# Feed-forward weights sent by GpSimd's DMA queue with a cast on the way, a fourth full set of exponentials, and another order

## The chip, the cores and the metric

The kernel runs on one core of a Trainium2 chip. The metric is the device time in microseconds of one launch, as the median of the runs shown; the profiled execution is a run of its own, with its own time. PE is TensorE, DVE VectorE, ACT ScalarE, POOL GpSimd and SP SyncE. The profile's "PEld" is TensorE's weight load, and "SPq" or "ACTq" stands for the DMA issues of that engine's queue.

## The reference

A chunk-selecting attention over 4 batches of 8 heads (768 positions, 64 dimensions a head) is followed by a feed-forward layer with a hard swish. Cut to what matters:

```python
k_min, k_max = chunks of 32 keys: min and max over each chunk
ub = sum over d of max(q * k_min, q * k_max)         # bound of each query on each chunk, causal
top_chunks = the 6 chunks with the largest bound
scores = q @ k.T / 8, kept where the chunk is chosen and the key is not later than the query
attn = softmax(scores) ; a = attn @ v                # float32 in and out
x = a with the 8 heads side by side                  # 3072 x 512
h = x @ w_in                                         # 512 x 2048
out = (h * clip(h + 3, 0, 6) / 6) @ w_out            # 2048 x 512
```

## The kernel before, in words

**Work units.** The 32 (batch, head) pairs are handled as 16 pairs of heads (i = 0 to 15, four to a batch), and from batch 1 on as six "quads" of four heads (n = 2 to 7). The feed-forward layer runs over eight groups g of 384 tokens, two to a batch. All the work is cut into tokens such as `S.1.3.b`, and a list of them, `ORDER`, is written out by hand: each token issues its instructions when its turn comes. Each engine runs its own instructions in the order of the list, and waits on semaphores for what it needs. A DMA is issued by the queue of the engine that is named for it, and stands in that engine's order too.

**Attention of batch 0** (capital letters). `LK`, `LQ`, `LV` load half pairs of k, q and v on SP's queue, `AK` and `AQ` some on ACT's. `KT` and `QT` transpose them on PE; `MX` and `MN` make the chunk bounds on DVE; `UH`, `UB`, `TH`, `T8`, `SE`, `LH`, `MT` make the mask rows from the six largest bounds. `EG` spreads a chunk indicator on POOL. `S.i.u` puts scores and mask of unit u (of six, line 23) of pair i into a two-bank PSUM tile, `ex` takes the exponential on ACT into a bf16 tile `PT`, `af` cuts the diagonal on POOL, `A` and `B` multiply with v, `na` and `nb` normalise on DVE into `XB`. `VC` casts v on POOL.

**Attention of batches 1 to 3.** `lk.n` and `lq.n` load a quad as four DMAs each into a third of `STAGE` in rows of 64 floats; `kd`/`qd` transpose 32 by 32 on DVE, `kb`/`qb` cast on ACT, `mx`, `mn`, `kx`, `rp` make the bounds' operands, `ud` the bounds on PE, `us`, `tr`, `tm`, `se`, `tb` the mask on DVE, `mv` gathers the mask rows on POOL (16 small copies a quad), `SQ` the scores.

**Feed-forward.** `X`/`xe` (batch 0) or `xt` (a transposing DMA) lay x out. `H.g.f` is 8 matmuls of 384 columns; it needs the 512 columns of w_in that hold f, that is chunk f // 2. `hu` (ACT) and `gt` (DVE) are the gate. `O.g.t.n` is 4 matmuls of 512 columns with chunk n of w_out; `ot` copies the result out on ACT and `st` stores it on SP. The last tile, g = 7 and t = 2, is `last_project`: two halves of 256 columns, each with its own copy and store; `st.7.1` is issued on SP behind them.

**Weights.** w_in and w_out come as eight chunks of 1 MB of float32 (n = 0 to 3 for w_in, 4 to 7 for w_out). `wl.n` (line 233) loads a chunk on SP's queue into one of two staging tiles `WS`, and `wc.n` (line 237) casts it on POOL into the bf16 matrices `WIN` and `WOUT`. A load waits for the cast two chunks before it, and a cast waits in POOL's order. The space of `WOUT` is lent to `RN` (line 198) while batch 0's bounds are made.

**Exponentials.** Three full sets of `PT` are tiles of their own. The fourth lies in the two `WS` tiles, and is used from pair 4 on, when the weights are cast; pairs 0 to 3 go round three sets (lines 182 to 188).

Of the kernel before, what the change touches and what calls it, by code (L numbers as in the profile page):

```python
# [39 lines left out]
SE.1.0 LH.1.0.a ex.0.0 MN.1.1 MX.1.1 MT.1.0 TH.2.0.y T8.2.0 SE.2.0 LK.0.1.1 KB.1.1 KT.0.1.x KB.0.1 LK.2.1.1 UH.1.1.a  # L40
LQ.0.1.1 UB.1.1 S.1.1.c ex.1.1 LK.2.1.0 KT.2.1.b KB.2.1 LQ.3.0.1 MN.0.1 LQ.0.1.0 QT.0.1.a MX.0.1 RA.0.1 LK.3.0.0
LK.3.0.1 LH.2.0.c QT.3.0.y QB.0.1 MT.2.0 MN.2.1 RP.0.1 RN.3.0 MX.2.1 LV.0.0.1 KT.3.0.x MN.3.0 QB.3.0 MX.3.0 S.2.1.c
RP.3.0 ex.2.1 af.2.1 LQ.2.1.1 S.1.0.a ex.1.0 UH.0.1.b LK.3.1.0 KB.3.0 TH.1.1.y LQ.2.1.0 UB.0.1 T8.1.1 SE.1.1 S.2.0.b
ex.2.0 UH.3.0.c QT.2.1.a RP.2.1 bd UB.3.0 RA.2.1 LQ.3.1.0 LQ.3.1.1 QT.3.1.x LH.1.1.c af.0.0 MT.1.1 QB.2.1 lk.2
TH.0.1.y S.1.3.b UH.2.1.c QB.3.1 af.1.0 ex.1.3 T8.0.1 SE.0.1 S.1.2.a ex.1.2 UB.2.1 RN.3.1 TH.3.0.y LH.0.1.c LV.0.0.0
MT.0.1 TH.2.1.b LK.3.1.1 T8.3.0 SE.3.0 S.0.3.c RP.3.1 ex.0.3 T8.2.1 S.0.2.a LV.1.0.0 ex.0.2 LH.3.0.y MT.3.0 KT.3.1.x
SE.2.1 MN.3.1 VC.0.0 A.0.y na.0 S.3.1.c af.1.2 ex.3.1 S.0.4.b ex.0.4 LV.1.0.1 VC.1.0 LV.3.0.1 MX.3.1 S.0.5.a ex.0.5
LH.2.1.c MT.2.1 af.1.1 LV.3.0.0 LV.2.0.1 A.1.y UH.3.1.c KB.3.1 na.1 LV.2.0.0 UB.3.1 S.2.5.b ex.2.5 af.0.2 VC.2.0
S.3.0.a kd.2.0 LV.0.1.1 ex.3.0 X.0.0.x VC.3.0 af.2.0 TH.3.1.y S.1.5.c ex.1.5 S.2.3.b ex.2.3 xe.0.0 T8.3.1 A.2.x
af.0.3 SE.3.1 S.1.4.a na.2 LV.0.1.0 S.2.2.c ex.1.4 LV.1.1.0 LH.3.1.x kd.2.1 MT.3.1 ex.2.2 af.0.5 VC.0.1 B.0.0.y  # L50
af.3.0 B.0.1.y nb.0 af.3.1 A.3.x LV.1.1.1 wl.0 LV.3.1.1 S.3.2.b na.3 ex.3.2 af.1.5 S.3.5.a ex.3.5 S.3.3.c X.0.1.y
xe.0.1 S.3.4.b ex.3.4 mn.2.0 af.1.3 VC.1.1 B.1.0.x B.1.1.x mn.2.1 ex.3.3 LV.2.1.1 nb.1 S.2.4.a ex.2.4 af.2.3 wc.0
H.0.0.b mx.2.1 LV.2.1.0 X.1.0.c VC.2.1 af.3.2 af.2.5 af.2.2 B.2.0.x mx.2.0 hu.0.0 af.3.5 LV.3.1.0 VC.3.1 gt.0.0
B.2.1.x wl.1 nb.2 af.3.3 B.3.0.y B.3.1.y H.0.1.b nb.3 X.1.1.x wc.1 kx.2 kb.2.1 xe.1.0 xe.1.1 hu.0.1 H.0.3.a gt.0.1
lk.3 kd.3.0 hu.0.3 gt.0.3 kd.3.1 H.1.3.c hu.1.3 H.1.2.b hu.1.2 gt.1.3 wl.2 H.0.2.a gt.1.2 wc.2 hu.0.2 H.0.5.c hu.0.5
mn.3.1 gt.0.2 gt.0.5 H.1.5.b hu.1.5 wl.3 wc.3 mx.3.1 H.0.4.a hu.0.4 H.0.7.c hu.0.7 gt.1.5 lq.2 kb.2.0 gt.0.4 kb.3.1
H.1.1.b hu.1.1 wl.4 wc.4 qd.2.1 rp.2.1 gt.0.7 qd.2.0 wl.5 rp.2.0 gt.1.1 mx.3.0 H.0.6.c hu.0.6 gt.0.6 mn.3.0 ud.2.b.a
O.0.0.0.y qb.2.0 us.2.1 us.2.0 O.0.2.0.x qb.2.1 tr.2.1 lq.3 H.1.6.b tr.2.0 hu.1.6 tm.2.1 tm.2.0 se.2.1 kx.3 wc.5
O.0.2.1.x tb.2.1 mv.2.3 H.1.4.a kb.3.0 hu.1.4 se.2.0 gt.1.6 O.0.0.1.y tb.2.0 qd.3.1 H.1.7.b rp.3.1 qd.3.0 rp.3.0
# [635 lines left out]
```

## Time and profile before

| what | value |
|---|---|
| median of 3 runs (range) | 274.97 us (274.05 to 279.04) |
| profiled execution, its own time | 274.82 us |
| its span, first to last instruction | 273.1 us |
| granted TensorE clock, mean | 0.997 |
| PE busy | 258.8 us, 95% of the span |
| DVE, ACT, POOL busy | 180.8, 180.4, 104.0 us |
| moved by DMA | 36.47 MB, 134 GB/s over the span |

Of the profiled execution's time, 1.7 us (274.82 less 273.1) lie outside the span. In the views, a row of windows gives the busy time of each engine in a stretch with the number of instructions in brackets, the granted clock, the DMA share (1 is all 16 engines busy; packets that overlap take it above 1) and GB/s. A row of the timeline gives start, length, engine, line and operation, and in square brackets the idle time before it with what ended it. A wait row gives the total in us, the number of times and the longest.

### The profile page before, as it was taken

What the parts mean: (1) busy time and instruction counts of PE and PEld (TensorE: products, weight loads), DVE (VectorE), ACT (ScalarE), POOL (GpSimd) and SP (SyncE); (2) the same over time, 40 slices, a digit from 0 to 9 for tenths busy, and PEclk for the clock granted to TensorE, in tenths of its full rate; (3) what the DMA queues carried; (4) which work ended last, traced back from release to release, by engine and by line L of the source; (5) the groups of instructions that cost most, each with busy time, mean ns of one, the idle gap of its engine ahead of it and who ended that gap; (6) DMA issues with size and microseconds to landing.
All of it is one profiled execution on the core that took longest, in us unless ns stands there. A gap on an engine that the chain in (4) does not pass through costs nothing.

```text
span 273.1 us, 8672 instructions
## 1 busy us (share of the span) xinstructions
PE 258.8 (95%) x3594; PEld 151.2 (55%) x3594; DVE 180.8 (66%) x450; ACT 180.4 (66%) x249; POOL 104.0 (38%) x243
## 2 busy tenths in 40 slices
PE   6899999779799999999999999999999999999994
PEld 2576786445444655755546754556565555555553
DVE  5998989979879596978866775555864212442340
ACT  3699984584499779958878673787577743435441
POOL 6525764424938756408354063322173120000000
PEclk9999999999999999999999999999999999999998
DMA  9978899999996957399912607540410240522103
GB/s 168 199 165 179 242 246 266 217 334 282 252 194 149 241 99 158 90 129 197 215 63 67 127 5 154 125 89 2 108 34 2 77 60 0 118 59 77 41 0 115
DMA packets 93111, 36.47 MB, mean 134 GB/s; under 512 B 85776, under 2 KB 86032, under 8 KB 93072
## 3 DMA queue, kind: packets, MB, share of 16 engines
q1 hardware_dynamic: 90672, 35.33, 58.7%
q10 hardware_dynamic: 2400, 0.59, 1.2%
q8 instruction: 28, 0.46, 0.8%
q14 instruction: 11, 0.09, 0.1%
HBM read 27.26 MB, written 6.29 MB: 123 GB/s over the span
## 4 chain that ended last, share of the span: by engine, by line
PE 71%; DMA 12%; SPq 4%; POOL 3%; DVE 3%; issue 2%; ACT 2%; ACTq 1%; DVEq 0%; POOLq 0%
PE PSy L627 15%; PE PSx L627 11%; PE PBc L590 10%; PE PBb L590 8%; DMA WS<-in_moe_w_in_dram 7%; PE PBa L590 6%; DMA STAGE<-in_q_dram 2%; PE PBc L513 2%; PE PBa L513 2%; SPq L217 2%; PE PSx L546 2%; SPq L392 2%; PE PBc L330 2%; PE PBb L513 2%; PE PSy L546 2%
## 5 line engine op out<-in xcount | busy, mean ns | idle before, releaser
L590 PEld LDWEIGHTS <-WIN 128*128 128x128 bf16 x512 | 48.8, 98 | 38.0 <-POOL WIN L237 2.7
L530 POOL TENSOR_SCALAR_AFFINE_SELECT PT<-PT 128x256 bf16<-128x256 bf16 x78 | 30.6, 414 | 73.7 <-ACT PT L523 73.1
L627 PEld LDWEIGHTS <-GT 128*128 128x128 bf16 x368 | 33.2, 98 | 38.9 <-issue 4.2
L627 PE MATMUL PSy<-WOUT,GT 128*128 128x512 bf16 x192 | 47.3, 380 | 0.0
L627 PE MATMUL PSx<-WOUT,GT 128*128 128x512 bf16 x160 | 39.9, 380 | 0.6 <-issue 0.6
L601 DVE SCALAR_TENSOR_TENSOR GT<-U,PBb 128x768 bf16<-128x768 bf16 x24 | 22.7, 944 | 21.6 <-ACT U L598 21.6
L590 PE MATMUL PBc<-XT,WIN 128*128 128x384 bf16 x184 | 33.7, 326 | 2.9 <-POOL WIN L237 1.6
L590 PE MATMUL PBb<-XT,WIN 128*128 128x384 bf16 x192 | 35.2, 326 | 0.0
L598 ACT ACTIVATE U<-PBb 128x768 bf16<-128x768 f32 x24 | 19.5, 814 | 20.4 <-PE PBb L590 20.3
L367 POOL COPY MQ<-MTM 32x144 bf16<-32x144 bf16 x96 | 29.3, 305 | 9.4 <-DVE MTM L362 5.5
L601 DVE SCALAR_TENSOR_TENSOR GT<-U,PBc 128x768 bf16<-128x768 bf16 x23 | 21.8, 947 | 14.5 <-ACT U L598 14.5
L523 ACT ACTIVATE PT<-PBa 128x1024 bf16<-128x1024 f32 (+2 forms) x28 | 27.3, 976 | 4.5 <-PE PBc L517 1.9
L598 ACT ACTIVATE U<-PBc 128x768 bf16<-128x768 f32 x23 | 18.7, 812 | 15.0 <-PE PBc L590 14.7
L523 ACT ACTIVATE PT<-PBc 128x1024 bf16<-128x1024 f32 (+2 forms) x28 | 24.2, 864 | 2.3 <-PE PBb L517 0.9
L523 ACT ACTIVATE PT<-PBb 128x1024 bf16<-128x1024 f32 (+2 forms) x22 | 20.8, 946 | 6.9 <-PE PBb L517 5.4
L590 PE MATMUL PBa<-XT,WIN 128*128 128x384 bf16 x136 | 24.9, 326 | 0.1
L223 DVE STREAM_TRANSPOSE STAGE<-STAGE 128x768 f32<-128x768 f32 x24 | 22.7, 958 | 2.0 <-DMA STAGE<-in_q_dram 1.7
L308 DVE TENSOR_REDUCE KMA<-STAGE 128x24 f32<-128x768 f32 x24 | 22.1, 942 | 0.1
L598 ACT ACTIVATE U<-PBa 128x768 bf16<-128x768 f32 x17 | 13.8, 814 | 10.6 <-PE PBa L590 10.6
L601 DVE SCALAR_TENSOR_TENSOR GT<-U,PBa 128x768 bf16<-128x768 bf16 x17 | 16.1, 948 | 6.6 <-ACT U L598 6.6
L546 PEld LDWEIGHTS <-PT 128*128 128x128 bf16 x546 | 18.9, 97 | 2.7 <-issue 0.2
L513 PEld LDWEIGHTS <-KBA 32*128 32x128 bf16 x480 | 9.2, 92 | 15.8 <-issue 12.4
(170 smaller groups left out, 443.5 us busy)
## 6 DMA issues: line engine op xcount, KB each, us to landing
...
```

The source lines that it names most:

```text
L217: nc.sync.dma_start(dst[CH * g:CH * (g + 1)], x[b, first + g].rearrange("(n t) d -> t n d", t=CH))
L223: nc.vector.transpose(out=T, in_=T)
L308: nc.vector.tensor_reduce(out=dst, in_=staged("k", n)[:, h], axis=AX.X, op=(A.max, A.min)[w])
L367: nc.gpsimd.tensor_copy(MQ[n % 2][CH * g:CH * (g + 1), w * part:w * (part + 1)], rows_of(n, g // 2)[CH * part:CH * (part + 1), w * (g % 2) ...
L513: nc.tensor.matmul(PSB[both[g // 2]][:, g % 2, at:at + w], lhsT=K[rows, x, j * P:(j + 1) * P], rhs=Q[rows, x, q0:q0 + w], start=(x == 0), ...
L523: nc.scalar.activation(pt(i, u)[:, :, 0:n], PSB[slot["S", i, u]][:, :, 0:n], ACT.Exp, scale=float(scale))
L530: nc.gpsimd.affine_select(out=T[:, :, lo:lo + P], in_=T[:, :, lo:lo + P], pattern=[[0, 2], [1, P]], compare_op=A.is_ge, fill=0.0, base=0, ...
L546: nc.tensor.matmul(O[:, e, t, :], lhsT=pt(i, u)[:, e, lo:lo + P], rhs=VB[i % 4][:, j, e, :], start=(j == 0), stop=(j == qb))
L590: nc.tensor.matmul(PSB[c][:, ff, 0:GRP], lhsT=WIN[:, kt, (2 * f + ff) * P:(2 * f + ff + 1) * P], rhs=XT[g % 3][:, kt, :], start=(kt == 0), ...
L598: nc.scalar.activation(slot["R", g, f][:], PSB[slot["H", g, f]][:, :, 0:GRP], ACT.Relu, bias=3.0)
L601: nc.vector.scalar_tensor_tensor(out=GT[g % 2][:, 2 * f:2 * f + 2, :], in0=slot["R", g, f][:], scalar=6.0, in1=PSB[slot["H", g, f]][:, :, ...
L627: nc.tensor.matmul(PSS[c], lhsT=GT[g % 2][:, f, t * P:(t + 1) * P], rhs=WOUT[:, f, :], start=(f == 0), stop=(f == FT - 1))
```

## The change

1. `load_w` issues its DMA on POOL's queue, from float32 in DRAM straight into `WIN` or `WOUT` in bf16: the DMA casts on its way. The `WS` tiles, `cast_w` and all `wc` tokens are gone.
2. `PT` is four full sets of tiles of their own, and pair i uses set i % 4 throughout.
3. `last_project` splits its 512 columns into 384 and 128 instead of 256 and 256.
4. `ORDER` is another list. The tokens are the same but for `wc`, with other places and other PSUM banks.

```diff
-    WS = ring(2, [P, 4, 512], FP32, "WS")
     COLS = [sum(x[3] for x in unit) for unit in UNITS]
-    PT = [[const.tile([P, 2, n], BF16, name=f"PT{i}_{u}")[:] for u, n in enumerate(COLS)] for i in range(3)]
-    spare = [t[:].rearrange("p a b -> p (a b)").bitcast(BF16) for t in WS]
-    SPARE = [(0, 0), (0, 1024), (0, 1536), (0, 2560), (1, 0), (1, 1024)]
-    PT.append([spare[w][:, at:at + 2 * n].rearrange("p (e n) -> p e n", e=2) for (w, at), n in zip(SPARE, COLS)])
-
+    PT = [[const.tile([P, 2, n], BF16, name=f"PT{i}_{u}")[:] for u, n in enumerate(COLS)] for i in range(4)]
     def pt(i, u):
-        return PT[i % 3 if i < NPAIR else i % 4][u]
+        return PT[i % 4][u]
...
     def load_w(n):
         c = n % 4
-        nc.sync.dma_start(WS[n % 2][:], wi[:, :, 512 * c:512 * (c + 1)] if n < 4 else wo[:, 4 * c:4 * c + 4, :])
-
-    def cast_w(n):
-        c = n % 4
-        nc.gpsimd.tensor_copy(WIN[:, :, 512 * c:512 * (c + 1)] if n < 4 else WOUT[:, 4 * c:4 * c + 4, :], WS[n % 2][:])
+        nc.gpsimd.dma_start(WIN[:, :, 512 * c:512 * (c + 1)] if n < 4 else WOUT[:, 4 * c:4 * c + 4, :],
+                            wi[:, :, 512 * c:512 * (c + 1)] if n < 4 else wo[:, 4 * c:4 * c + 4, :])
...
     def last_project(g, t, *banks):
         o, r = next_ot(), g * GRP + t * P
-        for h, c in enumerate(banks):
-            half = slice(256 * h, 256 * (h + 1))
+        for (lo, hi), c in zip(((0, 384), (384, 512)), banks):
             for f in range(FT):
-                nc.tensor.matmul(PSS[c][:, 0:256], lhsT=GT[g % 2][:, f, t * P:(t + 1) * P], rhs=WOUT[:, f, half],
+                nc.tensor.matmul(PSS[c][:, 0:hi - lo], lhsT=GT[g % 2][:, f, t * P:(t + 1) * P], rhs=WOUT[:, f, lo:hi],
                                  start=(f == 0), stop=(f == FT - 1))
-            nc.scalar.activation(o[:, half], PSS[c][:, 0:256], ACT.Copy, scale=1.0 / 6.0)
-            nc.sync.dma_start(out[r:r + P, half], o[:, half])
+            nc.scalar.activation(o[:, lo:hi], PSS[c][:, 0:hi - lo], ACT.Copy, scale=1.0 / 6.0)
+            nc.sync.dma_start(out[r:r + P, lo:hi], o[:, lo:hi])
```

Of the order, the parts that the prediction uses, as each engine sees them up to the first scores of quad 2 (its own tokens alone, in its order; "..." leaves tokens out):

```
DVE start   before  PW PT PO PF PZ MN.0.0 MX.0.0 RN.0.0 PR ...
            after   PR PZ PO PW PF PT MX.0.0 MN.0.0 MX.1.0 MN.1.0 ...
PE start    before  Z.c.6 KT.0.0 QT.0.0 KT.1.0 UH.0.0 ...
            after   Z.b.6 KT.0.0 KT.1.0 QT.1.0 QT.0.0 UH.1.0 UH.0.0 ...
POOL        before  PI PC PB EG x4 af.0.1 ... af.1.3 VC.1.1 af.2.3 wc.0 VC.2.1 ... af.3.3 wc.1 wc.2 wc.3 wc.4 wc.5
                    mv.2.3 mv.2.2 mv.2.1 wc.6 mv.2.0 wc.7 vc.4 ...
            after   PI PB PC EG x4 wl.0 af.2.1 ... af.1.5 af.3.3 af.3.2 af.3.5 wl.1 wl.2 wl.3 wl.4 wl.5 wl.6 wl.7
                    mv.2.1 mv.2.0 mv.2.3 mv.2.2 vc.4 ...
SP          before  ... lk.2 LV.0.0.0 ... wl.0 LV x4 wl.1 lk.3 wl.2 wl.3 lq.2 wl.4 wl.5 lq.3 wl.6 wl.7 lv.4 lk.4
            after   ... LV x8 lk.2 LV x8 lk.3 lq.2 lq.3 lv.4 lk.4 lq.4 ...
PE          before  ... S.2.4 H.0.0 X.1.0 B.2 B.3 H.0.1 X.1.1 H.0.3 H.1.3 H.1.2 H.0.2 H.0.5 H.1.5 H.0.4 H.0.7 H.1.1 H.0.6
                    ud.2 O.0.0.0 O.0.2.0 H.1.6 O.0.2.1 H.1.4 O.0.0.1 H.1.7 ud.3 O.0.0.2 SQ.2.3 O.0.2.2 O.0.0.3 SQ.2.2 O.0.2.3
            after   ... S.3.4 B.2 B.1 H.0.0 B.3 X.1.0 H.0.1 X.1.1 H.0.3 H.1.2 H.1.3 H.0.2 H.1.5 H.0.5 H.0.4 H.1.1 H.0.6
                    O.0.0.0 ud.2 O.0.2.0 H.0.7 H.1.4 H.1.6 O.0.2.1 O.0.0.1 ud.3 O.0.0.2 O.0.2.2 H.1.7 SQ.2.3 O.0.2.3 O.0.0.3 SQ.2.2
DVE         before  ... nb.1 mx.2 mx.2 gt.0.0 nb.2 nb.3 kx.2 xe.1.0 xe.1.1 gt.0.1 kd.3 gt.0.3 kd.3 ... qd.2.1 gt.0.7 qd.2.0 ...
            after   ... kx.2 kd.3 kd.3 nb.1 nb.0 nb.2 qd.2.0 xe.1.0 qd.2.1 nb.3 gt.0.1 xe.1.1 gt.0.0 ...
```

From quad 3 on, both lists carry the same tokens on each engine in a similar sequence, and both end with `O.7.2.0`, `ot.7.2`, `st.7.2`, `st.7.1`.

More of the change, by code (lines that the diff above doesn't have):

```diff
@@ L40 @@
[L40 to L59, printed above, removed]
@@ L105 @@
[L105 to L106 removed]
+PI PR PZ PO PW Z.b.6 PF PB PT AK.0.0.1 LK.0.0.0 KT.0.0.c MX.0.0 MN.0.0 LK.1.0.0 AK.1.0.1 AQ.1.0.0 KT.1.0.a MX.1.0
+AQ.1.0.1 MN.1.0 AQ.0.0.1 QT.1.0.b RN.1.0 AQ.0.0.0 PA KB.0.0 RP.1.0 QT.0.0.x RP.0.0 QB.1.0 RN.0.0 UH.1.0.c UB.1.0
+KB.1.0 LQ.0.1.0 LK.2.0.1 UH.0.0.b UB.0.0 TH.1.0.a T8.1.0 LK.2.0.0 KT.2.0.c LQ.2.0.0 MN.2.0 TH.0.0.b QB.0.0 LQ.2.0.1
@@ L107 @@
+hu.6.7 O.6.2.1.c gt.6.7 O.6.2.2.c H.7.3.b hu.7.3 gt.7.3 O.6.0.2.y O.6.0.3.y ot.6.0 O.6.1.3.x ot.6.1 st.6.0 st.6.1
+O.6.2.3.c ot.6.2 H.7.1.b hu.7.1 gt.7.1 st.6.2 H.7.0.a H.7.2.c hu.7.0 gt.7.0 hu.7.2 gt.7.2 H.7.7.b hu.7.7 H.7.4.a
+gt.7.7 O.7.0.0.y H.7.6.b hu.7.4 gt.7.4 hu.7.6 gt.7.6 H.7.5.c hu.7.5 O.7.0.1.y O.7.1.0.x O.7.1.1.x gt.7.5 O.7.0.2.y
+O.7.0.3.y ot.7.0 st.7.0 O.7.1.2.x O.7.1.3.x ot.7.1 O.7.2.0.a.c ot.7.2 st.7.2 st.7.1
 """.split()
```

119 lines of the change are left out of this document (66 added, 53 removed).

## The prediction

> **What bounds the kernel now.** I read the page first, for the busy shares, and then the windows, for the stretches in which PE is not busy.
>
> ```profile
> span 273.1 us, 8672 instructions
> PE 258.8 (95%) x3594; PEld 151.2 (55%) x3594; DVE 180.8 (66%) x450; ACT 180.4 (66%) x249; POOL 104.0 (38%) x243
> PE   6899999779799999999999999999999999999994
> DMA  9978899999996957399912607540410240522103
> ```
>
> ```profile
> core 0: us, PE busy (x) PEld busy (x) DVE busy (x) ACT busy (x) POOL busy (x), PEclk, DMA share, GB/s
> 0.00:2.00 2.00, 0.74 (x2) 0.28 (x3) 1.01 (x11) 0.00 (x0) 0.70 (x6) 1.00 0.02 4
> 2.00:12.00 10.00, 7.61 (x80) 4.44 (x82) 7.50 (x23) 5.14 (x12) 6.79 (x13) 1.00 1.18 217
> 12.00:30.00 18.00, 17.02 (x374) 12.30 (x368) 16.58 (x72) 17.38 (x32) 7.26 (x18) 1.00 0.77 168
> 30.00:76.00 46.00, 40.64 (x674) 26.56 (x671) 41.68 (x98) 29.42 (x38) 26.92 (x44) 1.00 1.09 269
> 44.00:46.00 2.00, 2.00 (x15) 1.20 (x13) 2.00 (x4) 0.81 (x1) 0.00 (x0) 1.00 0.99 369
> 260.00:273.10 13.10, 9.22 (x61) 5.72 (x59) 2.55 (x3) 3.59 (x6) 0.00 (x0) 0.94 0.17 60
> ```
>
> PE bounds the whole. It is idle for 273.1 - 258.8 = 14.3 us: 3.7 before 12 us (1.26 + 2.39), 1.0 up to 30, 5.4 from 30 to 76, 3.9 in the tail, and by subtraction 0.4 in the 184 us between 76 and 260. The change takes no matrix work away, so it can move these gaps and little else. Its subject lies in the 5.4 us: there the DMA engines are full (share 1.09) and DVE is 91% busy, so a late weight chunk is one cause among three. The next views are the waits for weights and the timeline around them.
>
> ```profile
> POOL WIN L237 <- DMA WS<-in_moe_w_in_dram: 9.3, 3, 3.8
> PEld L590 <- POOL WIN L237: 2.7, 3, 1.7
> 37.70 1.48 PE L590 MATMUL PBb<-XT,WIN 128*128 128x384 bf16 x8
> 43.19 4.99 PEld L590 LDWEIGHTS <-WIN 128*128 128x128 bf16 x32 [0.31 <-POOL WIN L237]
> 48.85 1.47 PE L590 MATMUL PBc<-XT,WIN 128*128 128x384 bf16 x8 [0.28 <-POOL WIN L237]
> 54.26 1.47 PE L590 MATMUL PBc<-XT,WIN 128*128 128x384 bf16 x8 [1.33 <-POOL WIN L237]
> 56.41 0.98 DVE L223 STREAM_TRANSPOSE STAGE<-STAGE 128x768 f32<-128x768 f32 x1 [1.65 <-DMA STAGE<-in_q_dram]
> 58.28 1.46 PE L590 MATMUL PBc<-XT,WIN 128*128 128x384 bf16 x8 [1.25 <-DVE GT L601]
> 70.91 1.89 POOL L237 CAST WOUT<-WS 128x2048 bf16<-128x2048 f32 x1
> 72.85 1.02 PE L627 MATMUL PSy<-WOUT,GT 128*128 128x512 bf16 x4
> 76.11 1.03 PE L627 MATMUL PSy<-WOUT,GT 128*128 128x512 bf16 x4
> ```
>
> The chunks of w_in cost PE 0.31 + 0.28 + 1.33 = 1.9 us. Then a load of q comes late, DVE waits 1.65 us for it, and a gate behind it holds PE for 1.25 us. Chunk 6 of w_out is cast to 72.80 us, and its first matmul starts at 72.85: the cast stood in POOL's order behind the mask copies of quad 2.
>
> **Removed: the casts and the staging.**
>
> ```profile
> L237 POOL CAST WIN<-WS x4: 1891/1894/1896, 34.2 to 52.3; 128x2048 bf16<-128x2048 f32 x4
> L233 SPq DMA_DIRECT2D WS<-in_moe_w_in_dram x4: 384/490/1325, 28.4 to 43.2; - x4
> DMA to landing us min/median/max: 5.5/7.7/9.4
> ```
>
> Eight casts of 1.89 us leave POOL (15 us), which is 38% busy, so nothing comes of that by itself. What counts is that a chunk is usable when it lands, 1.9 us sooner, and that a load no longer waits for a cast. The 1.9 us at the w_in chunks go: **-1.9 us**. On SP eight issues of about 0.5 us go, and lk.3, lq.2 and lq.3 no longer stand behind loads that wait for a cast. Of the later gaps (1.25 at 58.28, and the rest of the 5.4 us) I take back **-1.5 us**; at most it is 5.4 - 1.9 = 3.5, at least 0, since the DMA engines are full whoever issues.
>
> **Added: eight casting DMAs on POOL.** No row shows a DMA from POOL, nor one that casts. The time of the issue: from 0.38 us (shortest SP issue above) to 1.9 us (the cast that it replaces, as the nearest POOL row); I take 1. Behind wl.1 to wl.7 on POOL stand only the copies of `mv.2`:
>
> ```profile
> 38.84 0.41 POOL L530 TENSOR_SCALAR_AFFINE_SELECT PT<-PT 128x256 bf16<-128x256 bf16 x1
> 66.67 4.18 POOL L367 COPY MQ<-MTM 32x144 bf16<-32x144 bf16 x12 [3.02 <-DVE MTM L362]
> ```
>
> Those wait for DVE until 66.67 us; seven issues from about 38 us on, even at 1.9, end at 51. So the issue costs 0. Without this cover (POOL held for 4 us an issue, 38 + 28 = 66 us) `mv.2` and the scores of quad 2 would begin to slip. wl.0 is free on POOL behind the four EG copies, with af.2.1 next, several us later: 0.
>
> The time of the transfer decides more. At 44 us, with weights alone moving, the windows show 369 GB/s at share 0.99, so a 1.05 MB chunk takes 2.8 us of all engines. Rows of 256 bytes move at 217/1.18 = 184 GB/s: a chunk would take 5.7 us. Those are my two ends for a transfer that reads as much and casts. I take 2.8, since a chunk is still read in 2 KB rows, which is the row it is nearest to. Between wl.1 and the last chunk come also lq.3's 0.79 MB in small rows, 4.3 us. By plain rate the seven chunks and lq.3 take 7 x 2.8 + 4.3 = 24 us from 38 on: all landed at about 64. PE wants chunk 7 near 74 (76.11 less the gains). By the small-row rate they land at 38 + 7 x 5.7 + 4.3 = 82. The break-even is (74 - 38 - 4.3)/7 = 4.5 us a chunk.
>
> The Trainium skill, "SBUF — State Buffer" (in "SBUF: two separate sides", the box on the DVE-blocks-DMA trap), speaks against the change: a DMA issued by GpSimd has its descriptors written by GpSimd's cores, and a VectorE operation in a two-port mode locks them out until it ends. That would stretch the issues in a stretch where DVE is 91% busy. The L237 row speaks against it here: the casts, which by that page use the same port, ran beside that DVE and took 1891 to 1896 ns, without one stretched. By the rule, with every issue stretched, the sum would be that of the second rival; by the row, nothing. Its "DMA: Bandwidth & Descriptors" ("Anatomy of one DMA") gives 2.0 us plus bytes at 436 GB/s for such a DMA, an estimate of 4.4 us for a chunk, and by that the sum stays as it is; no run here shows it.
>
> **Moved: wl.1 and DVE's work.** wl.0 goes early, when the DMA share is 0.77, so 18 x 0.23 = 4 us of engine time are free for its 2.8. wl.1 goes late: on POOL it stands behind every af of batch 0. The last of these starts at 38.84 now; without the cast amid them, and with two exponentials fewer ahead, I put the issue at 38. The first matmul with chunk 1 (H.0.3) stands behind the same PE work in both orders, so PE comes to it near 43.2. The landing is 5.5 us at the shortest, 7.7 at the median: 43.5 to 45.7, a stall of 0.3 to 2.5. At the same place DVE now has kd.3 and qd.2, four transposes of 0.98 us, ahead of xe.1.1, which H.1.2 needs; gt.0.0 (0.9) moves behind it. That is +3 us on an engine with 1.4 us to spare between 12 and 30, and it needs lq.2 on time. Both stalls run at once, and the moved transposes are missing later, where they hold gates now (58.28). I take **+1.5 us** for both, between 0.3 and 3.
>
> **Moved: the start.**
>
> ```profile
> 0.93 0.27 DVE L243 MEMSET XT<- 128x256 uint32 x1 [0.93 <-PEq L679]
> 1.08 0.29 POOL masks.py:199 TENSOR_SCALAR_AFFINE_SELECT IDENT<-IDENT 128x128 f32<-128x128 f32 x1
> 1.21 0.33 DVE L250 MEMSET KMA<- 128x64 f32 x4
> 1.53 0.23 DVE L252 MEMSET VB<- 128x12 bf16 x4
> 2.64 0.70 DVE L281 MEMSET EM<- 128x768 uint32 x1
> 3.31 0.18 DVE L282 MEMSET BIAS<- 128x144 f32 x1
> 6.47 0.22 DVE L258 CAST IDENTB<-IDENT 128x128 bf16<-128x128 f32 x1
> 1.26 2.74 PE L289 MATMUL PBc<-XT 128*128 128x512 bf16 x6 [1.26 <-DVE TINY L246]
> 4.68 1.02 DVE L416 TENSOR_REDUCE KMA<-PSx 128x12 f32<-128x384 f32 x2 [1.19 <-PE PSx L402]
> ```
>
> PE's six warming matmuls wait for WARM's memset. It now comes behind PR, which waits for the identity (1.37 us), and the memsets of EM, BIAS4, KM and VB: 1.4 + 0.22 + 0.70 + 0.18 + 0.33 + 0.23 + 0.27 = 3.3 us. The matmuls end near 6.1, and DVE's first reduction comes near 6.7, not 4.68: 2 us late. But DVE has done PR and the memsets by then that it does in between now, and the k and q that PE waits for by 6.5 have landed. Of the 10 us from 2 to 12 DVE is idle for 2.5 now; the after lies at 2.6 between 4.1 and 6.7 and next to nothing behind. I take **+0.5 us**, between 0 and 2.
>
> **The fourth set and the tail.** A separate fourth set frees pair 3 from waiting for pair 0's values; ACT is idle for 0.6 us in 12 to 30, so it is worth 0 to 0.6, and I take 0.
>
> ```profile
> 265.72 1.75 PE PBb L616 x16
> 269.25 0.38 ACT L618 ACTIVATE OT<-PSy 128x256 f32<-128x256 f32 x1 [1.36 <-PE PSy L616]
> 270.05 0.42 SPq L638 DMA_DIRECT2D out_dram<-OT  x1
> ```
>
> Sixteen matmuls of 256 columns take 1.75 us, so 512 columns take 3.5 in either split. The last copy shrinks from 256 to 128 columns, 0.38 to about 0.27, and st.7.1 still goes out last: **-0.1 us** (0 to -0.4).
>
> **The sum**, on the profiled execution's 274.8: -1.9 - 1.5 + 1.5 + 0.5 - 0.1 = -1.5, so **273.3 us**. That execution lies 0.15 below the median of 274.97, which I neglect. A measurement of this kernel can tell about 2% (5.5 us) from no change.
>
> **The rivals.** First, *the gaps close altogether*: the 5.4 us of 30 to 76 go, and the start costs nothing: 274.8 - 5.4 = 269.4. For it: the weights leave SP and the casts go. Against it: a DMA share of 1.09, and 41.68 us of DVE in 46, which no edit makes less. It only just passes 2% (269.5).
>
> Second, on the other side, *the casting transfer is slow*: each chunk takes over 4.5 us (the break-even), by its rate or because POOL is locked out while it writes them. At 5.7 us the last lands at 82 against a need at 74, 8 us of PE, with 2 to 3 more at the chunks before, as H.0.6 and O.0.0.0 follow each other at once: 273.3 + 10 = 283. For it: full DMA engines, and the small-row rate. Against: rows of 2 KB and 10 us of slack.
>
> Third, *the order's front stalls*: lq.2 lands late under the weights, DVE stands at qd.2 with nb.3 and the gates behind it, and H.1 with them. One late load of q cost DVE 1.65 and PE 1.25; four DMAs so late, with chunk 1 at its 2.5: 273.3 + 4 = 277.
>
> **The chances.** Forecast 0.48, third rival 0.20 (it holds most of "the same"), second 0.24, first 0.08. Low end 269: all of 30 to 76 gained, and a little of the tail. High end 284: the second rival at its rate. Beyond them I leave about 0.13, most of it above. The likeliest case alone has 270 to 276. Faster by over 2%: 0.06, most of the first. Slower by over 2% (280.5): 0.29, the second and a quarter of the third. The same: 0.65.
>
> **What would show it.** In the changed profile: wl.0 issued near 9 to 10 us and wl.1 near 38; PE's waits for WIN under 2.5 us; PE idle in 30 to 76 of 3 to 5 us; first scores' work 0 to 2 us later at 12 us; PE busy still near 259. It is wrong if the chunks land over 4.5 us apart, if `mv.2` waits for POOL rather than for DVE, or if a gap of over 1 us opens behind 80 us.

## The result and the profile after

The changed kernel takes 286.17 us (median of 4 runs, 285.71 to 286.84) against 274.86 us for the kernel before on the same chip: a ratio of 1.042, with a 95% interval of 1.039 to 1.046. It is 4% slower; 273.3 us were forecast, and the range ended at 284. The profiled execution took 286.53 us. Medians of the kernel before lie between 274.9 and 277.8 us in the sets of runs below, so each experiment is given as a ratio to its own set. A ratio leaves out runs more than 1.5% above the fastest of their kernel; of the kernel with wl.0 late, below, these are two of four (285.2 and 285.4 us, beside 280.6 and 281.7).

The page of the changed kernel: shares, slices, queues and issues.

```profile
span 284.8 us, 8655 instructions
...
PE 262.7 (92%) x3594; PEld 152.6 (54%) x3594; DVE 182.7 (64%) x450; ACT 180.4 (63%) x249; POOL 93.8 (33%) x243
...
PE   5778997994799979999999999999999999999994
...
PEclk9989999999599999999999999999999999999999
DMA  9999689999059287874970235095310220502002
...
q1 hardware_dynamic: 86448, 26.95, 45.4%
q0 software_dynamic: 4224, 4.19, 9.3%
...
WIN<-in_moe_w_in_dram POOLq DMA_DIRECT2D x4, 512.0 KB, 7.0
WOUT<-in_moe_w_out_dram POOLq DMA_DIRECT2D x4, 512.0 KB, 16.8
```

Two DMA queues matter now: q1 is SP's, with the rows of q, k and v, and q0 is POOL's, with the weights. Slices 10 and 11 (64 to 78 us) are the ones to look at: PE is busy for 4 tenths of the first, beside full DMA engines, and in the second the clock is at 5 tenths and the DMA engines at 0.

The same windows as before, of the changed kernel:

```profile
0.00:2.00 2.00, 0.00 (x0) 0.00 (x0) 0.51 (x2) 0.00 (x0) 1.21 (x9) 1.00 0.02 4
2.00:12.00 10.00, 7.89 (x61) 4.90 (x62) 6.26 (x27) 3.66 (x8) 7.04 (x12) 1.00 1.08 188
12.00:30.00 18.00, 14.75 (x291) 9.92 (x289) 14.35 (x60) 14.04 (x29) 4.68 (x13) 0.91 0.97 190
30.00:76.00 46.00, 37.73 (x584) 25.61 (x584) 36.99 (x84) 28.87 (x36) 14.59 (x31) 0.94 0.93 159
76.00:110.00 34.00, 31.71 (x590) 16.92 (x588) 25.69 (x76) 24.94 (x35) 19.32 (x53) 0.98 0.74 144
260.00:284.80 24.80, 20.96 (x127) 11.62 (x125) 6.68 (x7) 9.20 (x14) 0.00 (x0) 1.00 0.18 64
```

and one of the kernel before:

```profile
76.00:110.00 34.00, 33.94 (x541) 17.98 (x539) 25.72 (x67) 29.35 (x40) 21.27 (x58) 1.00 0.85 166
```

The span grew by 284.8 - 273.1 = 11.7 us. PE is idle 22.1 us in place of 14.3, which is 7.8 of it: by the rows, +0.5 before 12 us, +2.3 from 12 to 30, +2.9 from 30 to 76, and +2.2 from 76 to 110 (34 - 31.71, against 0.06 before). The other 3.9 us are PE busy with the same matmuls: the granted clock is below 1 in three of these rows and was 1.00 in them before.

The largest hole, in the changed kernel's timelines of DVE and PE:

```profile
71.88 0.98 DVE L218 STREAM_TRANSPOSE STAGE<-STAGE 128x768 f32<-128x768 f32 x1 [7.30 <-DMA STAGE<-in_q_dram]
73.26 1.76 PE L582 MATMUL PBa<-XT,WIN 128*128 128x384 bf16 x5 [6.11 <-DVE UBM L331]
```

In its waits (total, times, longest):

```profile
DVE STAGE L218 <- DMA STAGE<-in_q_dram: 10.4, 2, 7.3
PE PBa L582 <- DVE UBM L331: 6.1, 1, 6.1
POOL MQ L359 <- DVE MTM L354: 45.3, 6, 27.2
```

And the four loads of lq.3 by their line, with the time of their issues and from issue to landing:

```profile
L212 SPq DMA_DIRECT2D STAGE<-in_q_dram x4: 312/572/8952, 50.0 to 51.6; - x4
...
DMA to landing us min/median/max: 10.7/17.4/20.2
```

lq.3 is issued at 50.0 to 51.6 us and its last piece lands 20.2 us later, at 71.8. DVE stands 7.3 us at its transpose (qd.3), the bounds of quad 2 stand behind it in DVE's order, and PE waits 6.1 us for the PSUM tile that they hold. No wait for a weight chunk is left, neither of PE nor of POOL.

What the DMA engines did meanwhile, in 2 us each:

```profile
50.00:52.00 2.00, 2.00 (x18) 1.29 (x16) 2.00 (x4) 0.74 (x2) 0.00 (x0) 1.00 1.25 206
60.00:62.00 2.00, 2.00 (x14) 1.23 (x13) 1.42 (x3) 1.46 (x3) 0.00 (x0) 1.00 1.22 196
68.00:70.00 2.00, 0.00 (x0) 0.00 (x0) 0.00 (x0) 0.00 (x0) 0.00 (x0) 1.00 1.37 192
70.00:72.00 2.00, 0.00 (x0) 0.00 (x0) 0.12 (x1) 0.00 (x0) 0.00 (x0) 0.55 0.60 87
```

At 50 us weights move alone, at 206 GB/s as written in bf16, twice that as read. At 60 us the share and the sum are the same, but two queues have a part in it. Counting the trace's single packets by queue gives how the engines divided themselves:

```
changed kernel        q0 (weights)             q1 (rows of lq.3)
50 to 52 us           418 packets,  95 ns      none
56 to 58 us           311 packets,  94 ns      310 packets, 31 ns
60 to 62 us           319 packets,  92 ns      320 packets, 30 ns
64 to 66 us           321 packets,  92 ns      321 packets, 30 ns
68 to 70 us            10 packets             1490 packets, 29 ns
```

One packet for one: a row packet carries 256 bytes and a weight packet 1 KB, so each row waits for 94 ns of weights. The rows get 0.079 MB in 2 us, 39 GB/s, where the windows before the change showed 184 GB/s of such rows; alone at 68 us they get 188. Four pieces of 0.197 MB at 39 GB/s take 20 us, which is what the landing row says.

### The profile page after: what moved, and what is told of

The parts are those of the page before. It is cut to its first block, busy times and chain, and to the rows that moved or that the text cites. A ratio compares the mean times of both kernels' runs of the same rounds, so it can differ in the third digit from the quotient of the medians.

```text
span 284.8 us, 8655 instructions
## 1 busy us (share of the span) xinstructions
PE 262.7 (92%) x3594; PEld 152.6 (54%) x3594; DVE 182.7 (64%) x450; ACT 180.4 (63%) x249; POOL 93.8 (33%) x243
## 4 chain that ended last, share of the span: by engine, by line
PE 72%; DMA 12%; DVE 6%; SPq 4%; issue 2%; ACT 2%; POOL 0%; DVEq 0%; POOLq 0%; ACTq 0%
PE PSy L618 12%; PE PSx L618 11%; DMA STAGE<-in_q_dram 11%; PE PBa L582 9%; PE PBb L582 9%; PE PBc L582 6%; SPq L212 3%; PE PBb L505 2%; PE PSy L538 2%; PE PSx L538 2%; DVE STAGE L218 2%; PE PBa L505 2%; PE PBc L505 1%; PE PBc L322 1%; PE PBc L618 1%
## 5 line engine op out<-in xcount | busy, mean ns | idle before, releaser
L522 POOL TENSOR_SCALAR_AFFINE_SELECT PT<-PT 128x256 bf16<-128x256 bf16 x96 | 37.1, 411 | 82.1 <-ACT PT L515 75.3
L618 PE MATMUL PSx<-WOUT,GT 128*128 128x512 bf16 x176 | 43.2, 380 | 0.0
L618 PE MATMUL PSy<-WOUT,GT 128*128 128x512 bf16 x176 | 43.2, 380 | 0.0
L582 PE MATMUL PBa<-XT,WIN 128*128 128x384 bf16 x176 | 33.5, 335 | 6.1 <-DVE UBM L331 6.1
L515 ACT ACTIVATE PT<-PBb 128x1024 bf16<-128x1024 f32 (+2 forms) x34 | 32.1, 944 | 4.8 <-PE PBb L509 1.9
L515 ACT ACTIVATE PT<-PBc 128x1024 bf16<-128x1024 f32 (+2 forms) x32 | 29.3, 916 | 8.9 <-PE PBc L509 6.6
L593 DVE SCALAR_TENSOR_TENSOR GT<-U,PBa 128x768 bf16<-128x768 bf16 x22 | 20.8, 947 | 14.0 <-ACT U L590 13.9
L582 PE MATMUL PBc<-XT,WIN 128*128 128x384 bf16 x160 | 29.3, 326 | 0.0
L590 ACT ACTIVATE U<-PBa 128x768 bf16<-128x768 f32 x22 | 17.8, 811 | 14.8 <-PE PBa L582 9.9
L538 PEld LDWEIGHTS <-PT 128*128 128x128 bf16 x672 | 22.8, 97 | 3.5 <-issue 0.5
```

What stands on the lines that cost most here:

```text
L515: nc.scalar.activation(pt(i, u)[:, :, 0:n], PSB[slot["S", i, u]][:, :, 0:n], ACT.Exp, scale=float(scale))
L522: nc.gpsimd.affine_select(out=T[:, :, lo:lo + P], in_=T[:, :, lo:lo + P], pattern=[[0, 2], [1, P]], compare_op=A.is_ge, fill=0.0, base=0, ...
L538: nc.tensor.matmul(O[:, e, t, :], lhsT=pt(i, u)[:, e, lo:lo + P], rhs=VB[i % 4][:, j, e, :], start=(j == 0), stop=(j == qb))
L582: nc.tensor.matmul(PSB[c][:, ff, 0:GRP], lhsT=WIN[:, kt, (2 * f + ff) * P:(2 * f + ff + 1) * P], rhs=XT[g % 3][:, kt, :], start=(kt == 0), ...
L590: nc.scalar.activation(slot["R", g, f][:], PSB[slot["H", g, f]][:, :, 0:GRP], ACT.Relu, bias=3.0)
L593: nc.vector.scalar_tensor_tensor(out=GT[g % 2][:, 2 * f:2 * f + 2, :], in0=slot["R", g, f][:], scalar=6.0, in1=PSB[slot["H", g, f]][:, :, ...
```

## The experiments

Every ratio is to the kernel before on the same chip, with its 95% interval. Edits of the order are written as the tokens moved.

**lq.3 or wl.0 out of the weights' way, each alone and both.** The first kernel makes POOL wait for lq.3 before it sends wl.4:

```diff
- ... wl.3 hu.0.4 wl.4 ... ud.2 lq.3 ...
+ ... wl.3 hu.0.4 lq.3 hq.3 wl.4 ...        # hq.3: POOL copies one column of lq.3's tile
```

> The changed kernel, with the issues of the four w_out chunks held on GpSimd until the q rows of quad 3 (lq.3) have landed: a copy of one column out of those rows stands ahead of wl.4, and lq.3 stands ahead of it in the list (its place on SP's queue stays). Theory A (the burst of seven chunks on a ring of its own starves lq.3, the small rows that share the engines): lq.3 lands 5 to 10 us after its issue, not 20; DVE's wait of 7.3 us and PE's of 6.1 us near 70 us go, and with them the half clock behind: 286 less 6 to 9, so 277 to 280. Theory B (a casting transfer is slow in itself): the w_out chunks then land later than 75 us and PE waits for them; the time stays at 284 to 290. Theory C (the order of DVE and PE ahead of quad 2 is what costs): the stall moves by less than 2 us, 284 to 287.

Ratio 1.026 (1.020 to 1.032), span 280.5. lq.3 lands at 55.2 to 59.9 us and the 6.1 us hole is gone, but wl.4, sent only at 60.5, is now late: in this kernel's waits stands

```profile
PE PSy L622 <- DMA WOUT<-in_moe_w_out_dram: 4.3, 1, 4.3
```

Four tenths of the loss come back; the rest of what lq.3 gained is given away again at w_out. The second kernel sends wl.0 behind the fourth v cast of batch 0, at 27.9 us in place of 9.4:

```diff
- ... S.1.1.a wl.0 SE.0.1 ...
+ ... VC.3.0 wl.0 ex.1.3 ...
```

> The changed kernel, with the first weight chunk (wl.0) moved on GpSimd from behind the EG copies (issued at 9.4 us) to behind VC.3.0 (about 30 us). Theory A' (its transfer shares the engines with the first q and k halves, whose landing went from a median of 2.6 to 6.3 us): landings back to about 3 us, H.0.0 2 to 3 us earlier than 44.1, total 283 to 284.5. Rival (the start is late because the warming matmuls come late and the halves are loaded in another order): under 1 us, 285.5 to 286.5. If it does no good because the chunk then lies in the way of lk.2 and the v halves, it is 286 or more.

Ratio 1.015 (1.008 to 1.023), span 278.9, more than I had thought. The loads of q and k issued from 9 to 12 us, by line, of the changed kernel:

```profile
DMA to landing us min/median/max: 2.0/6.3/6.6
```

of this one:

```profile
DMA to landing us min/median/max: 2.5/2.6/2.9
```

and this one's window:

```profile
12.00:30.00 18.00, 15.77 (x336) 10.97 (x333) 16.49 (x78) 16.41 (x32) 6.33 (x15) 1.00 0.79 166
```

At the median, one chunk of 1 MB beside these rows makes them land in 6.3 us where 2.6 do without it. PE gets 15.77 us of work in 12 to 30 at a full clock, in place of 14.75 at 0.91. The hole at qd.3 stays, at 4.3 us. The third kernel makes both edits and puts PE's warming matmuls first again:

```diff
- PI PR PZ PO PW Z.b.6 PF ...
+ PW Z.b.6 PI PR PZ PO PF ...                # and wl.0 and hq.3 as above
```

> The changed kernel with three edits at once: the w_out chunks held until lq.3 has landed, wl.0 behind VC.3.0, and the memset of WARM with the six warming matmuls first, as before the change. If the three causes are the burst, the early chunk and the late start, this takes back nearly all of the 11.3 us: 273 to 277. If the rest of the order costs, it stays at 278 to 282.

Ratio 1.028 (1.021 to 1.035): a miss. PE was warmed at 1.3 to 4 us, but its matmuls took the longer time of a lower clock until 20.6 us:

```profile
16.02 0.90 PE L398 MATMUL PSy<-IDENT,STAGE 128*128 128x128 f32 x3
20.57 0.56 PE L398 MATMUL PSy<-IDENT,STAGE 128*128 128x128 f32 x3
```

The clock column of the windows stands at 1.00 there all the same. PE had gaps of 1.4 and 0.8 us behind the warm-up, but that they are the cause isn't shown: of the kernels of the old order below, which start with the same instructions as the kernel before, the traces record the full clock first at 9.0 to 9.5 us in three, at 13.3 and 20.7 us in two, and at 5.3 us in the kernel before itself. On top came 2.1 us ahead of X.1.1 and 3.0 us of waiting for w_out.

**lq.3 in the weights' ring.** Sent by POOL, in line between wl.3 and wl.4, lq.3 cannot meet a weight packet of the other queue:

```diff
-                nc.sync.dma_start(dst[CH * g:CH * (g + 1)], ...
+                queue = nc.gpsimd if (m, n) == ("q", 3) else nc.sync
+                queue.dma_start(dst[CH * g:CH * (g + 1)], ...
```

> The changed kernel with one edit: the four DMAs of lq.3 are issued on GpSimd's queue, between wl.3 and wl.4, instead of on SP's. The bytes and the burst are the same; the rows now stand in one ring with the weights and go in turn, not packet against packet. Theory A'' (two rings share each engine packet by packet, so a 256 B row pays for a 1 KB weight packet each time): lq.3 lands within 10 us of its issue (before 60 us) and DVE's 7.3 us wait goes; 278 to 281. Rival (the rows are late since the engines have more bytes to move than time, in whatever order): lq.3 lands no earlier than 66, and the time stays at 284 to 287. If GpSimd needs several us for the descriptors of so many rows, wl.4 is late and PE waits for w_out: 281 to 286.

Ratio 1.018 (1.009 to 1.027), span 278.0. The same four loads by line, sent by POOL in this kernel:

```profile
L212 POOL DMA_DIRECT2D STAGE<-in_q_dram x4: 723/728/747, 49.1 to 51.2; - x4
...
DMA to landing us min/median/max: 8.4/8.9/9.3
```

8.9 us in place of 17.4, though they still stand behind two chunks of w_in. The hole, and the half clock behind it, are gone. What is left over 0.5 us from 30 to 76 us is 2.2 us ahead of X.1.1 and 0.9 at w_out.

**The packets by themselves.** To test one-for-one turns directly, each chunk of w_out goes in two halves of 256 columns, and nothing else changes. A weight packet then has 512 bytes:

```diff
+            for at in range(0, 512, 256):
+                nc.gpsimd.dma_start(WOUT[:, 4 * c:4 * c + 4, at:at + 256], wo[:, 4 * c:4 * c + 4, at:at + 256])
```

> The changed kernel with one difference: each of the four chunks of w_out goes as two casting DMAs of 256 columns, so that a packet is 512 bytes in place of 1 KB, and lq.3 shares the engines with twice as many packets of half the size. POOL issues four DMAs more, 3 us. Theory (the engines alternate between the two rings packet by packet): each row packet waits for a weight packet of about half the time (some 50 to 60 ns in place of 94), so the rows of lq.3 move at 45 to 50 GB/s in place of 39 and land near 67 to 69 us in place of 71.8; the idle stretch of 6.1 us shrinks to 3 to 5 us, while w_out's last chunk lands no sooner than before (70 us or later). Ratio 1.025 to 1.04. Rival (rows and weights share the engines by bytes, or the rows are late for a reason of their own): lq.3 lands at 71 us or later and the stretch stays at 6 us or more, ratio 1.04 or above.

```
half packets          q0 (weights)             q1 (rows of lq.3)
58 to 60 us           494 packets,  57 ns      494 packets, 30 ns
64 to 66 us           492 packets,  58 ns      493 packets, 30 ns
```

```profile
L211 SPq DMA_DIRECT2D STAGE<-in_q_dram x4: 312/596/5346, 51.5 to 53.1; - x4
...
DMA to landing us min/median/max: 8.3/12.5/16.3
```

Ratio 1.024 (1.013 to 1.035). Again one for one, and with a weight packet of 58 ns the rows get 0.122 MB in 2 us, 61 GB/s, above the 45 to 50 I expected. They land in 12.5 us at the median instead of 17.4, and the hole shrinks from 6.1 to 2.3 us. Four tenths of the loss come back by cutting packets that nobody waits for; sharing by bytes would have changed nothing.

**The transport alone.** The old order with the casting DMAs, `wl` at their old places:

```diff
-        nc.sync.dma_start(WS[n % 2][:], ...                   # load_w, before
+        nc.gpsimd.dma_start(WIN[...] if n < 4 else WOUT[...], ...   # as in the changed kernel; cast_w empty
```

> The kernel before with one part of the change alone: the eight weight DMAs are issued on GpSimd, casting, and the casts are left out; the order is that of before (so GpSimd issues wl.1 to wl.5 in a burst near 39 us, wl.6 and wl.7 behind the copies of mv.2), and the two staging tiles stay only as the fourth set of exponentials. Theory A (burst against small rows): lk.3, lq.2 or lq.3 land late, DVE waits for them, 277 to 283. Theory B (slow cast): PE waits for the chunks themselves, 280 to 290. Theory C (the new order alone is the cause): 273 to 276.

Ratio 1.038 (1.031 to 1.046), mainly by two late chunks. wl.0 goes out at 35.9 and PE waits 2.8 us; wl.6 and wl.7 stand on POOL behind `mv.2`, at 72.7 and 76.1, and PE's timeline has

```profile
82.35 1.01 PE L627 MATMUL PSy<-WOUT,GT 128*128 128x512 bf16 x2 [6.27 <-DMA WOUT<-in_moe_w_out_dram]
```

So these places belong to the old transport. With these two right behind wl.5:

```diff
- ... wl.5 rp.2.0 ... mv.2.2 wl.6 qb.3.1 ... mv.2.0 wl.7 ...
+ ... wl.5 wl.6 wl.7 rp.2.0 ... mv.2.2 qb.3.1 ... mv.2.0 ...
```

> e4_cast_old_order with wl.6 and wl.7 moved on GpSimd from behind the mask copies of mv.2 to right behind wl.5, so that PE does not wait for w_out for that reason (6.3 us in e4). The old order, then, with all of the casting transport. Theory A'': lq.2 and lq.3 now meet seven chunks, and DVE waits 5 us or more for them in all; ratio 1.015 to 1.035. If e4 was slow by its two late chunks alone: 1.00 to 1.01.

Ratio 1.012 (1.004 to 1.021); the 4.3 us for wl.0's chunk stay. With wl.0 behind the first v cast too, at 26.3 us:

```diff
- ... VC.0.0 A.0 ... LV.1.1.1 wl.0 LV.3.1.1 ...
+ ... VC.0.0 wl.0 A.0 ... LV.1.1.1 LV.3.1.1 ...
```

> The order of the kernel before with the casting transfers, the last two weight chunks sent right behind wl.5 (1.0124), and now wl.0 sent from POOL behind the first v cast, near 26 us, in place of 34.7. Theory: the casting transfers cost nothing by themselves; what they cost in the old order was wl.0 landing at 42.7, with 4.3 us of idle TensorE and 3.4 us of half clock behind it. Then both go, some 5 us less: ratio 0.985 to 1.003. Rival: the second ring takes as much from the loads of k and v around 26 to 34 us as the late wl.0 did: another idle stretch of 2 us or more before 45 us, ratio 1.008 or more.

Ratio 1.006 (1.000 to 1.012), this kernel's window being

```profile
30.00:76.00 46.00, 40.91 (x688) 27.06 (x685) 41.52 (x96) 29.57 (x38) 17.76 (x42) 1.00 1.19 196
```

PE's 40.91 is what the kernel before has there, 40.64. The ratio lies between the two expectations: in these places the transport costs 0.6%, by the interval something from nothing to 1.2%, and brings nothing. Two further kernels of this kind, wl.1 at 27.7 us as well, and then lq.2 and lq.3 on POOL:

```diff
+ ... VC.1.0 wl.1 LV.3.0.1 ...                  # both
+ ... gt.1.3 lq.2 wl.2 ... kb.2.0 lq.3 ... wl.4 ...   # the second, with queue = nc.gpsimd for these rows
```

> The old order with casting transfers, wl.0 near 26 us (1.006), and now wl.1 right behind it, near 27 to 28 us. Theory: the transport is free when its chunks are sent into DMA time that the start leaves over; the 1.6 us stretch at 44.5 us (wl.1 landed at 46.0) goes and lq.2, which shared with five chunks, meets one less; ratio 0.995 to 1.004. Rival: what wl.1 takes from k and v at 28 to 36 us comes back as a later X.0.1 or H.0.0: ratio 1.006 or more.

> As the kernel before in this list, and lq.2 and lq.3 sent by POOL, lq.2 ahead of wl.2 and lq.3 ahead of wl.4: everything that meets the weights stands in one ring. Theory: rows land in turn, nothing in 30 to 76 us waits for them, the stretches of 1.0 to 1.3 us at 58 and 70 us that the old order has may stay: ratio 0.985 to 1.002. Rival: POOL, which has to wait for the rows' buffers before it goes on to its masks and weight issues, becomes the wait: TensorE or ACT stand for POOL over 1 us, ratio 1.005 or more.

Ratios 1.006 (1.000 to 1.012) and 1.044 (1.038 to 1.050). In the first the stretch at 44.5 us is gone, but PE is idle for 3.1 us at 56.8, where DVE waits for a load of q. The second is a miss that my rival had right: POOL reached lq.3 and stood at its buffer,

```profile
POOL STAGE L217 <- ACT KBA L300: 13.5, 1, 13.5
```

with w_out's chunks behind it, and PE lost 6.3 us to them at 67.8. (It is also the kernel whose full clock came at 20.7 us, so a part of its loss lies at the start.) One ring is a cure only where the rows' buffer is free when POOL comes to it.

**The order alone.** The new order with SP's loads, the staging and POOL's casts. The places of the weights in SP's queue are mine, and pair 3's exponentials lie in the tile of a gate that isn't used yet. First with four chunks ahead of lq.2, then with two:

```diff
+ SP, first   lk.2 ... wl.0 wl.1 lk.3 wl.2 wl.3 lq.2 wl.4 wl.5 lq.3 wl.6 wl.7
+ SP, second  wl.0 lk.2 ... lk.3 wl.1 lq.2 wl.2 wl.3 lq.3 wl.4 wl.5 wl.6 wl.7
```

> The new order with the old transport: weights on SP's queue into two staging tiles and cast on GpSimd, with wl and wc set among the new order's tokens as they lie in the old one (wl.0 and wl.1 ahead of lk.3, wl.3 ahead of lq.2, wl.6 and wl.7 behind lq.3, the casts ahead of their first use). Pair 3's exponentials lie in the second gate buffer, which is free then; the last tile is split 384 and 128. Theory A'' (the transport is the cause): ratio to the kernel before 0.99 to 1.01. Rival C (the order is the cause): 1.02 to 1.04, with DVE at qd.2 and qd.3 the place.

> The new order with the transport of before (SP, staging, casts on POOL), as in the order-alone kernel (1.0432), but the rows lk.3 and lq.2 now stand ahead of wl.2 and wl.3 in SP's queue, wl.0 is sent near 28 us, and lq.3 goes ahead of wl.4. Theory: the new order is no dearer than the old as long as its rows are early; qd.2 then waits under 2 us and the ratio is 0.995 to 1.015. Rival: the order is dear by itself (it wants lq.2 some 5 us sooner than the old one while two staging buffers hold the weights back): the ratio stays above 1.025, with idle stretches before X.1.1 or the second weight chunk.

Ratios 1.043 (1.034 to 1.053) and 1.037 (1.023 to 1.051). In the first, X.1.1 waits 6.5 us, since DVE stands at qd.2 for lq.2; in the second 2.9, with two holes of 2.0 and 2.2 us at 35 and 42 us and 10.2 us of half clock. I found no place for the weights in SP's queue that this order bears. That it bears none is not shown.

**The rest of the new order.** The one-ring kernel with a late wl.0, then lq.2 sent by POOL as well:

```diff
+ ... VC.3.0 wl.0 ex.1.3 ...                                     # both
+                queue = nc.gpsimd if m == "q" and n in (2, 3) else nc.sync   # the second
```

> The changed kernel with two moves: lq.3 is sent by POOL in line behind wl.3 (as in the one-ring kernel, 1.0176), and wl.0 is sent behind the fourth v cast, near 28 us, in place of 9.4 us. Theory: two rings sharing the engines packet by packet is the whole cost, at both places. Then the first q and k halves land in 2.5 us again, H.0.0 starts near 41.7 us as with the late wl.0 (44.1 in the changed kernel), the 2.2 us idle stretch ahead of X.1.1 shrinks below 1.5, and the ratio to the kernel before is 1.000 to 1.012. Rival: the new order of the work costs something by itself, whatever the rings do: the ratio stays at 1.015 or more, with TensorE idle where no DMA is late.

> The one-ring kernel with the late wl.0 (1.010, interval 0.991 to 1.029), with one difference: lq.2 too is sent by POOL, in line ahead of wl.1, so no row of lq.2 meets a weight packet of the other ring. Theory: the 3.3 us idle stretch ahead of X.1.1 (lq.2's last piece landed at 47.2 beside wl.1) and the 3.4 us of half clock behind it go, about 4 us less; ratio 0.992 to 1.006. Rival: the new order itself costs what is left; TensorE stands as long at other places with no DMA late, ratio 1.008 or more.

Ratios 1.010 (0.991 to 1.029) and 1.017 (1.008 to 1.027). In both the hole ahead of X.1.1 grew, against what I expected: to 3.3 and 3.9 us. From the timelines of DVE and PE of the first:

```profile
47.29 0.98 DVE L218 STREAM_TRANSPOSE STAGE<-STAGE 128x768 f32<-128x768 f32 x1 [1.75 <-DMA STAGE<-in_q_dram]
...
49.71 0.56 DVE L558 TENSOR_TENSOR XB<-PSx,RINV 128x384 bf16<-128x384 f32 x1
...
50.32 0.49 PE L571 MATMUL PSx<-IDENTB,XB 128*128 128x128 bf16 x6 [3.27 <-DVE XB L558]
```

The division that X.1.1 needs (nb.3) is ready on DVE but stands behind two transposes of lq.2, which lands at 47.2. An earlier start brings PE sooner to X.1.1, and lq.2 is no sooner. On POOL lq.2 is even later, as POOL comes to it only at 41.9. So the last kernel moves just these two transposes:

```diff
- nb.2 qd.2.0 X.1.0 xe.1.0 H.0.1 hu.0.1 qd.2.1 nb.3 gt.0.1 X.1.1 xe.1.1 gt.0.0
+ nb.2 X.1.0 xe.1.0 H.0.1 hu.0.1 nb.3 gt.0.1 X.1.1 xe.1.1 gt.0.0 qd.2.0 qd.2.1
```

> The one-ring kernel with the late wl.0 (1.010), with one difference in the order: the two turns of lq.2 on DVE (qd.2.0, qd.2.1) stand behind the division, copies and gates of the first pair (nb.3, xe.1.0, gt.0.1, xe.1.1, gt.0.0) in place of ahead of them. Theory: what is left of the loss is the order's place for these turns, since nb.3 waits on DVE behind qd.2.1 for lq.2 and X.1.1 with it (3.3 us, then 3.4 us at half clock). Then the stretch before X.1.1 falls under 0.5 us, the clock stays full from 40 to 60 us, and the time falls by 4 us or more: ratio 0.990 to 1.004. Rival: the turns and the kb.2.1 and rows of lq.3 behind them only come later and the stall moves to the second weight chunk or to qd.3: TensorE idle of 2 us or more elsewhere in 48 to 76 us, ratio 1.008 or more.

Ratio 1.009 (1.005 to 1.014), with the windows

```profile
12.00:30.00 18.00, 15.75 (x336) 10.97 (x333) 16.48 (x78) 16.38 (x32) 6.33 (x15) 1.00 0.85 170
30.00:76.00 46.00, 41.15 (x694) 27.30 (x691) 41.30 (x85) 29.65 (x38) 20.96 (x48) 1.00 0.99 169
76.00:110.00 34.00, 31.25 (x532) 16.30 (x531) 25.75 (x75) 27.36 (x36) 18.99 (x50) 1.00 0.80 160
```

The hole before X.1.1 is gone, and 30 to 76 us is better than before the change (41.15 us of PE against 40.64, at a full clock). The rival had the ratio right all the same: what this kernel still loses lies elsewhere, 1.3 us in 12 to 30 and 2.7 in 76 to 110. There PE is idle for 2.24 us at 93.4, and the profile names nothing that it waited for:

```profile
95.67 0.30 PE L322 MATMUL PBc<-STAGE,KMA 32*32 32x144 f32 x1 [2.24 <-issue]
```

Six of the twelve kernels of the new order have such a stretch, of 1.7 to 2.2 us (the changed kernel's is 1.8 us at 100.8), no kernel of the old order has one, and it always falls among the 128 small matmuls of `ud.4`. The traces hold one thing that goes with it, a 16 KB packet of the queue that the page of the profile lists as q8, "instruction". In all six it starts 0.8 to 0.9 us after the first of these matmuls, and PE stops 0.9 to 1.0 us after the packet's start; in the other six it starts 2.7 to 3.2 us ahead of them. So PE may have stood there for its own instructions; no run moves this packet alone, so that isn't shown.

A variant before these, with wl.0 late, kb.2.1 earlier, and w_out held from wl.5 on:

```diff
+ ... VC.3.0 wl.0 ... B.3.0 kb.2.1 hu.0.0 lq.2 ... hu.0.4 lq.3 wl.4 ... qb.3.1 hq.3 wl.5 ...
```

> The changed kernel with three edits: wl.0 behind VC.3.0 (as in e2_wl0_late), kb.2.1 ahead of hu.0.0 on ACT so that lq.3 is free to issue 3 us sooner, and the hold for lq.3 ahead of wl.5 rather than wl.4, so that wl.4 is not late for O.0.0.0. The late warming is kept. Theory A'': no wait for a q load over 3 us, PE's waits for w_out under 2 us, no stretch at half clock near 70 us: ratio to the kernel before 0.99 to 1.005 (272 to 276 on this kernel's usual scale). If the rest of the order costs by itself, 1.01 to 1.02.

Ratio 1.020 (1.011 to 1.030), another miss: wl.1 was sent at 41.1, lq.2's last piece landed at 49.9 instead of about 47 us, and X.1.1 waited 6.2 us. No version beat the kernel before.

## Why the prediction was wrong, step by step

Where the time goes shows when both kernels are compared at the same place in PE's work. In the profiled executions these tokens start at (us; what PE has done by a place is the same in all four, within five weight loads):

```
                 before   changed        wl.0 late      lq.3 in one ring
H.0.3             43.2    50.2  +7.0     48.8  +5.6     49.7  +6.5
ud.2              60.1    62.9  +2.8     61.5  +1.4     63.5  +3.4
ud.4              89.9    99.0  +9.1     95.3  +5.4     91.5  +1.6
ud.5             117.5   129.3 +11.8    123.5  +6.0    121.7  +4.2
end of the span  273.1   284.8 +11.7    278.9  +5.8    278.0  +4.9
```

**The step that failed** is the term for the meeting of lq.3 and the weights: "By plain rate the seven chunks and lq.3 take 7 x 2.8 + 4.3 = 24 us ... all landed at about 64. PE wants chunk 7 near 74". The total was about right: from 43.7 to 71.8 us is 28. But it asked only when the last chunk lands, as though rows and weights left in the order in which they were issued. In one ring lq.3 lands in 8.9 us. With two rings the engines take a packet of each in turn, the rows, put at 4.3 us, took up to 20.2 to land, and the one that came late was lq.3, which PE wanted near 67. From ud.2 to ud.4 the changed kernel falls back by 6.3 us (2.8 to 9.1), where the kernel with lq.3 in one ring gains 1.8. The third rival had this mechanism, a load of q late "under the weights, DVE stands at" its transpose with the gates behind it, but it looked at lq.2 and priced it at 4 us; lq.3's hole is 6.1, with 3.8 us of half clock behind it. With its chance of 0.20 it should have been weighed from two rings, at both places where rows and weights meet.

The Trainium skill, "DMA: Bandwidth & Descriptors" ("Queues, rings and completion order"), says that a DMA engine goes round between the rings it has work for and changes at packet boundaries. The counts 310 to 311 and 494 to 494 agree, if a record of the trace is what the page calls a packet.

**The way to H.0.3** is the second step. The prediction had PE come to it "near 43.2", and with +0.5 for the start and +1.5 for the front the loss there would be 2.0 us. It is 7.0: PE is idle 4.7 us more up to there (0.5 before 12 us, 2.3 from 12 to 30, 1.9 behind 30), and the rest is the same work at a lower clock (half from 19.0 to 22.4 us, and the full clock first recorded at 8.8 us, in the kernel before at 5.3).

wl.0 was priced at 0, with "4 us of engine time" free for it. The free time was an average over 12 to 30; the chunk went out at 9.4, into a stretch that had a share of 1.18 in the kernel before. Sent late, it gives back 2.7% (1.042 to 1.015), but little of that at the start: the feed-forward layer starts 2.4 us sooner (41.7 in place of 44.1) and H.0.3 only 1.4. Of the 5.9 us between the two spans, 2.3 more are lq.3's smaller hole, with a shorter half clock, and 2.1 lie between ud.4 and ud.5, where this kernel lacks the 1.8 us stretch. (The same holds for the 4.3 us of the kernel that holds w_out: it too lacks that stretch.) The other 5.6 us at H.0.3 stay when wl.0 is late; no run takes them apart.

**The clock** was no term at all. PE busy was to stay near 259 and is 262.7.

**Right**: the removal of the waits at w_in and part of the later gaps (no wait for a chunk is left, and from H.0.3 to ud.2 the loss shrinks by 4.2 us, where -1.9 and -1.5 were forecast; 0.31 of the -1.9 is a wait of the weight load, not of PE); the casting transfer at the large-row rate (2.8 us a chunk taken; the chunks that move alone land 2.5 and 2.6 us apart, at 49.05, 51.59 and 54.21, and those beside lq.3 3.3 to 4.5, without a wait of PE); the issue at 1 us (0.75 to 0.88 measured) and hidden, as `mv.2` waits for DVE; the stall at the front of H (1.4 us ahead of X.1.1, 1.9 from 30 us to H.0.3, +1.5 forecast); the idle time before 12 us (+0.5 forecast, +0.5); the tail (3.8 us idle against 3.9). **Wrong by size**: wl.1 went out at 43.7, not 38, and no stall came of it, since PE came to H.0.3 at 50.2; PE's idle time from 30 to 76 us, 8.3 us where 3 to 5 were to show it. The gap that I named as a sign of error "behind 80 us" did open, the 1.8 us at 100.8.
